# VectorE's queue in the code's order between the first and the second MoE

## The chip, the cores and the metric

The kernel runs on one core of one Trainium2 chip. The metric is the device time of one execution in microseconds (us), the median of several runs. A core has five engines with a queue each: TensorE (PE, matrix products), VectorE (DVE), ScalarE (ACT), GpSimd (POOL) and SyncE (SP, which here issues nearly all transfers). Each engine takes the instructions of its own queue one after the other, and an instruction that waits for another engine holds up what is queued behind it on the same engine.

## The reference

Four sequences of 448 positions go through attention with 12 heads of width 64, then every token through two feed-forward blocks (called MoE in the code). All tensors are float32.

```python
q_n, k_n = rmsnorm(q, g_q), rmsnorm(k, g_k)            # per head, over the 64 columns
attn = softmax(q_n @ k_n.T / sqrt(64))                 # 448 x 448
x = (attn @ v) laid out as (4 * 448 tokens, 768)
g = relu(x @ w_in) ** 2                                # w_in 768 x 2048
x = g @ w_out                                          # w_out 2048 x 768
a, b = x @ w1, x @ w2                                  # 768 x 1024
out = ((a * b) @ w3) @ moe2_w_out                      # 1024 x 1024, 1024 x 768
```

The weights arrive in 64-bit floats; the first use of each makes its float32 form on the chip and stores it for the later batches.

## The kernel before

**Numbers.** A float32 operand is held as a high part and a low part, and a product is three TensorE passes (`mm3`, L399 to L401: high by high, high by low, low by high). So every weight block ("unit", 128 x 384 or 128 x 512) and every activation needs a copy for the high part (ACT, L134) and a subtraction for the low part (POOL or DVE, L141).

**Loop over heads.** The body handles batch after batch. Iteration h of `for h in range(NH + 1)` (48 heads) emits, in this order: the first half of the scores of head h (`stage_qk`: four products, two row maxima L922 and their product L923 on DVE), exponentials on ACT (`stage_exp`, L939), transposes of the probabilities of head h-1 on PE (`stage_t`) with high parts on ACT and low parts on DVE (`stage_lo`), the parts of v (`v_prep`, vhl), the second half of the scores, the product with v (`stage_v`, its DVE sum is L1026), in every fourth iteration the norms of the next group of four heads (`group_prep`: square on ACT, sum over columns on DVE L843, then a short chain over DVE and ACT), and the operands of head h+2 (`head_prep`: kx, khl, qh, ql). Every second head ends in `stage_x` (L1032), which makes a block of the MoE's input.

**MoE work in between.** Between those stages `fill(n)` emits n TensorE passes of a running generator. In iterations 0 to 12 (batch 0's attention) that is a product of two weights (`gen_w3o`), in iterations 13 to 24 (batch 1's attention) it is `gen_moe(0)`, the MoE of batch 0, and from there on `gen_late`, the MoE of batches 1 and 2. At the end of iteration 24 the first MoE is emitted to its end by `fill(1e9)`. In the first MoE the weights are the 64-bit ones: a load of 384 or 512 KB into one of 4 buffers (raw64; SP, L309), two instructions that cut the words out (ACT L323 and POOL L329), one on DVE that joins them into float32 (L336, "join", into one of 6 raw buffers, which frees the raw64 buffer), then the high part on ACT (into one of 4 + 2 hl buffers), the low part, which frees the raw buffer, and a store of the float32 form. In the emitted order, `use(u)` emits beside the products of unit u: the load of unit u+9, the words of u+7, the join of u+6, the high part of u+5 and the low part of u+4 (`advance`, with SPLIT_AHEAD, WORD_AHEAD, JOIN_AHEAD, HI_AHEAD). The last part of the first MoE (`w3o`, 144 of its 1008 passes) needs no joins. Results of a product are taken from PSUM by a callback right after the last pass: `relu2` (r and act on ACT, gf on DVE L474, act's low part on DVE L141), `add` (L501), `gated` (L528).

**What sets the order.** The program is traced in the emitted order; a scheduler then orders every engine's queue itself, by its own estimates of when things are ready. Where the code has called `in_order(engines)`, `chain()` adds for these engines an ordering edge (it makes no wait on the chip) from each instruction to the one emitted before it on that engine, until the next call of `in_order`; the first one of such a stretch is put behind the last 300 before it. Instructions emitted after the stretch are not tied by it and may be put between. Before the change there are two stretches: SP from the end of iteration 24 on, and all five engines from the last half of the last MoE on.

Of the kernel before, what the change touches and what calls it, by code (L numbers as in the profile page):

```python
# [30 lines left out]
def attention_moe_kernel(  # L31
# [16 lines left out]
    SP, ACT, DVE, POOL, PE = (e.engine for e in (nc.sync, nc.scalar, nc.vector, nc.gpsimd, nc.tensor))  # L48
# [65 lines left out]
    def in_order(*engines):  # L114

        spans.append((nc.cur_bb.bb.instructions[-1], engines))
# [655 lines left out]
    def load_group(g):  # L772
        if not (0 <= g < NH // GH):
            return
        b, h0 = divmod(g * GH, H)
        qn = t1.tile([P, GH, C, D], F32, name="qn", tag="qn")
        kn = t2.tile([P, GH, C, D], F32, name="kn", tag="kn")
        if g == 0:
            nc.sync.dma_start(out=kn[:, 0:1], in_=k_nat[0, :, 0:1])
            load_head(0)  # L780
            nc.sync.dma_start(out=qn[:, 0:1], in_=q_nat[0, :, 0:1])
            load_to(0)
            nc.sync.dma_start(out=kn[:, 1:], in_=k_nat[0, :, 1:GH])
            nc.sync.dma_start(out=qn[:, 1:], in_=q_nat[0, :, 1:GH])
            load_to(1)
        else:
            nc.sync.dma_start(out=kn, in_=k_nat[b, :, h0:h0 + GH])
            nc.sync.dma_start(out=qn, in_=q_nat[b, :, h0:h0 + GH])
        grp[g] = [qn, kn, None, None]

    def load_head(h):
        if not (0 <= h < NH):
            return
        b, hh = divmod(h, H)
        t = t2.tile([128, S], F32, name="qt", tag="qt")
        nc.sync.dma_start(out=t, in_=q_t[b, hh])
        qts[h] = t

    def load_v(h):
        if not (0 <= h < NH):  # L800
            return
        b, hh = divmod(h, H)
        t = t2.tile([128, C, D], F32, name="v", tag="v")
        nc.sync.dma_start(out=t, in_=v_in[b, hh])
        vs[h] = t
# [103 lines left out]
    def stage_qk(h, s):  # L909
        if not (0 <= h < NH):  # L910
            return
        d = heads[h]
        nb = d["nb"] = small.tile([P, 2], F32, name="nb", tag="nb")
        c0 = 2 * s
        o = d["sc"] = [None, None]
        for j in range(2):
            c = c0 + j
            ps = ps_sc.tile([128, 512], F32, name="sc", tag="sc")
            o[j] = ps[:P, :S]
            nc.tensor.matmul(o[j], d["qh"][:, c * P:(c + 1) * P], d["kt"], start=True, stop=False)  # L920
            nc.tensor.matmul(o[j], d["ql"][:, c * P:(c + 1) * P], d["kt"], start=False, stop=True)  # L921
            nc.vector.tensor_reduce(out=nb[:, j:j + 1], in_=o[j], axis=AX.X, op=ALU.max, negate=True)  # L922
        nc.vector.tensor_tensor(out=nb, in0=nb, in1=d["rq"][:, c0:c0 + 2], op=ALU.mult)  # L923

    def stage_exp(h, s):
        if not (0 <= h < NH):
            return
        d = heads[h]
        nb, o = d.pop("nb"), d.pop("sc")
        i = h % 2  # L930
        if s == 0 and i == 0:
            sums2[h // 2] = small.tile([P, 2, C], F32, name="sm", tag="sm")
        sm = sums2[h // 2]
        c0 = 2 * s
        pp = t3.tile([P, 2, S], F32, name="p", tag="p")
        for j in range(2):
            c = c0 + j
            p = d["p"][c] = pp[:, j, :]
            nc.scalar.activation(  # L939
                out=p, in_=o[j], func=AF.Exp, scale=d["rq"][:, c:c + 1], bias=nb[:, j:j + 1],  # L940
                accum_out=sm[:, i, c:c + 1],
            )
        if h >= H:
            words = t3.tile([P, 2, S], F32R, name="pw", tag="pw")
            nc.sync.dma_start(out=words.bitcast(F32), in_=pp)
            d["p"][c0:c0 + 2] = [words[:, 0, :], words[:, 1, :]]
        if s == 1 and i == 1:
            nc.vector.tensor_scalar(out=sm, in0=sm, scalar1=1e-9, scalar2=None, op0=ALU.add)
            rs = small.tile([P, 2, C], F32, name="rs", tag="rs")
            nc.vector.reciprocal(out=rs, in_=sm)  # L950
            wide = t1.tile([P, C, 2, D], F32, name="rsw", tag="rsw")
            nc.gpsimd.tensor_scalar(
                out=wide, in0=rs.rearrange("p i c -> p c i").unsqueeze(3).to_broadcast([P, C, 2, D]),
                scalar1=1.0, scalar2=1.0, op0=ALU.mult, op1=ALU.mult,
            )
            sums2[h // 2] = wide.rearrange("p c i d -> p c (i d)")

    def stage_t(h, kc):
        if not (0 <= h < NH):
            return  # L960
        d = heads[h]
        k0, kn = KCS[kc]
        ps = ps_pt.tile([128, 512], F32, name="pt", tag="pt")
        to, one = (ps.bitcast(F32R), ident_r) if h >= H else (ps, ident)
        for c in range(C):
            nc.tensor.transpose(to[:kn, c * P:(c + 1) * P], d["p"][c][:, k0:k0 + kn], one)  # L966
        if kn == 128:
            t = t3.tile([128, 2, S], F32R, name="ptr", tag="ptr", bufs=3)
            hi, lo = t[:, 0, :], t[:, 1, :]
            d["pt"][kc] = [hi, lo]  # L970
        else:
            t = t1.tile([128, S], F32R, name="pte", tag="pte")
            hi, lo = t[:kn, :], t[kn:, :]
            d["pt"][kc] = [t]
        copy_on("a", hi, ps[:kn, :S])
        d["lo"].append((lo, ps[:kn, :S], hi.bitcast(F32)))
# [51 lines left out]
    def stage_x(h):  # L1028
        if 0 <= h < NH and h % 2:
            x = xf[0]  # L1030
            b, hh = divmod(h, H)
            nc.vector.tensor_tensor(out=x, in0=norms_to_rows(h), in1=x, op=ALU.mult)  # L1032
            late = b == B - 1 and hh // 2 in (2, 3, 4)
            t = (x2p if late else xp).tile([128, 2, S], F32R, name="x", tag="x2" if late else "x")
            copy_on("a", t[:, 0, :], x)
            sub_on("g", t[:, 1, :], x, t[:, 0, :].bitcast(F32))
            xs[b, hh // 2] = t
# [4 lines left out]
    def start_fill(gen, total):  # L1042
        state.update(gen=gen, credit=0.0, left=total)

    def fill(n):
        state["credit"] += n
        while state["gen"] is not None and state["credit"] > 0:
            try:
                k = next(state["gen"])
                state["credit"] -= k  # L1050
                state["left"] -= k
            except StopIteration:
                state["gen"] = None
# [29 lines left out]
    for h in range(NH + 1):  # L1083
        n = W3O / ((H + 1) * 6) if h <= H else (MOE / (H * 6) if h <= 2 * H else (MOE + IN) / (2 * H * 6))
        late = h > 2 * H
        if not late:
            load_head(h + 3)
            load_v(h + 1)
            if h % GH == 0:
                load_group(h // GH + 1)  # L1090
        stage_qk(h, 0)
        fill(n)
        stage_exp(h, 0)
        if late:
            load_head(h + 3)
            load_v(h + 1)
            if h % GH == GH - 1:
                load_group((h + 1) // GH + 1)
        if h % H != 1:
            stage_x(h - 2)  # L1100
        stage_t(h - 1, 0)
        stage_t(h - 1, 1)
        fill(n)
        stage_lo(h - 1)
        if h < NH:
            v_prep(h)
        fill(n)
        even = H <= h
        if even:
            stage_qk(h, 1)  # L1110
        stage_k(h + 1)
        stage_t(h - 1, 2)
        stage_t(h - 1, 3)
        fill(n)
        stage_lo(h - 1)
        if not even:
            stage_qk(h, 1)
            fill(n)
        stage_exp(h, 1)
        fill(n)  # L1120
        if even:
            fill(n)
        stage_v(h - 1)
        if h >= 2 * H and h % GH < 2:
            group_prep(h // GH + 1, "qk"[h % GH])
        elif h % GH == 1:
            group_prep(h // GH + 1)
        head_prep(h + 2)
        if h and h % H == 0:
            if h != 3 * H:  # L1130
                fill(1e9)
            stage_x(h - 1)
            if h == H:
                start_fill(gen_moe(0), MOE)
            elif h == 2 * H:
                in_order(SP)
                start_fill(gen_late(), MOE + IN)
            elif h == NH:
                start_fill(gen_pair(), MOE)
# [58 lines left out]
```

## Time and profile before

| | us |
|---|---|
| runs | 1225.1, 1224.67, 1230.58 (median 1225.1) |
| the profiled execution, its own time | 1222.35 |
| its span, first to last instruction | 1220.6 |
| busy in the span: PE | 1157.7 (95%) |
| weight loads of PE | 1036.3 (85%) |
| DVE | 856.2 (70%) |
| ACT | 728.1 (60%) |
| POOL | 719.2 (59%) |

The rows further down come from one profiled execution; times in them count from the start of its span. A busy PE is not a PE at its peak, because passes overlap: back to back, a pass of 448 columns starts about every 0.2 us and is shown with 0.36 us. The granted clock (PEclk) is 1.00 for 2.4 GHz and 0.50 for 1.2 GHz. A row of a timeline has the start, the duration, the engine, the line, the operation, output and inputs by the program's names, and in square brackets the idle time of that engine before it with the instruction that ended it. For one core, this execution is the only one shown, and its own time stands 2.75 us under the median of the runs.

### The profile page before, as it was taken

The numbers are of one execution on the slowest core, as the hardware profiler recorded it, in microseconds if no ns is written. First come the engines' busy times: TensorE is split into PE (matmuls) and PEld (weight loads), VectorE is DVE, ScalarE is ACT, GpSimd is POOL, SyncE is SP. The second block draws the span as 40 slices with busy tenths as digits, with TensorE's granted clock in tenths as the row PEclk, the third lists the DMA queues.
The fourth block names the chain that finished last, engine by engine and source line by source line (L and its number), as shares of the span: only waits on it lengthen the run. The fifth ranks groups of instructions, "written<-read, shape, count | busy, mean of one in ns | idle before, by whom it ended". The sixth has DMA issues, their size and how long they took to land.

```text
span 1220.6 us, 19049 instructions
## 1 busy us (share of the span) xinstructions
PE 1157.7 (95%) x6150; PEld 1036.3 (85%) x6150; DVE 856.2 (70%) x1441; ACT 728.1 (60%) x1586; POOL 719.2 (59%) x720
## 2 busy tenths in 40 slices
PE   7799999898898899999999999999999999999998
PEld 4588888787786789998989988889989999889998
DVE  5799879868987792766787666677564311887786
ACT  6799877767655655665664565665654535343352
POOL 6775534655675665765786756485665958521132
PEclk9699999999898999999999999999999999999999
DMA  7785648799877754565474655655545656243333
GB/s 229 233 254 162 190 129 265 244 296 265 275 243 238 233 160 152 151 196 154 148 215 133 210 156 182 206 170 168 166 139 178 188 161 193 93 124 106 121 104 117
DMA packets 122435, 224.15 MB, mean 184 GB/s; under 512 B 13440, under 2 KB 75104, under 8 KB 122336
## 3 DMA queue, kind: packets, MB, share of 16 engines
q1 hardware_dynamic: 120608, 220.19, 59.2%
q10 hardware_dynamic: 1728, 2.75, 0.6%
q8 instruction: 48, 0.79, 0.3%
q14 instruction: 51, 0.42, 0.1%
HBM read 157.03 MB, written 36.96 MB: 159 GB/s over the span
## 4 chain that ended last, share of the span: by engine, by line
PE 47%; DVE 10%; DMA 6%; ACT 4%; issue 2%; POOL 2%; SPq 0%; ACTq 0%; DVEq 0%; POOLq 0%
PE mm L399 11%; PE mm L400 11%; PE mm L401 11%; PE kv L1018 2%; PE pt L966 2%; DMA raw<-w 2%; DMA raw<-f_out 1%; DVE vhl L138 1%; DVE nb L922 1%; POOL hl L141 1%; ACT p L939 1%; PE pt L400 1%; PE pt L401 1%; PE sc L401 1%; PE sc L399 1%
## 5 line engine op out<-in xcount | busy, mean ns | idle before, releaser
L141 POOL TENSOR_TENSOR hl<-raw,hl 128x384 fp32r<-128x384 f32 (+1 forms) x317 | 372.4, 1182 | 240.1 <-ACT hl L134 210.6
L134 ACT ACTIVATE hl<-raw 128x384 fp32r<-128x384 f32 (+1 forms) x405 | 225.7, 566 | 194.0 <-PE mm L401 40.1
L400 PE MATMUL mm<-x,hl 128*128 128x448 f32 (+1 forms) x640 | 235.5, 368 | 8.9 <-POOL x L141 8.9
L399 PE MATMUL mm<-x,hl 128*128 128x448 f32 (+1 forms) x640 | 239.5, 374 | 4.6 <-DVE gf L474 2.9
L401 PE MATMUL mm<-x,hl 128*128 128x448 f32 (+1 forms) x640 | 234.1, 366 | 0.0
L400 PE MATMUL mm<-act,hl 128*128 128x448 f32 (+1 forms) x544 | 200.8, 369 | 3.5 <-POOL act L141 3.5
L399 PE MATMUL mm<-act,hl 128*128 128x448 f32 (+1 forms) x544 | 202.9, 373 | 0.0
L401 PE MATMUL mm<-act,hl 128*128 128x448 f32 (+1 forms) x544 | 198.8, 366 | 0.0
L939 ACT ACTIVATE p<-sc,nb,rr 112x448 f32<-112x448 f32 x192 | 137.5, 720 | 97.1 <-DVE nb L923 96.7
L400 PEld LDWEIGHTS mm<-x,hl 128*128 128x128 f32 x640 | 121.7, 190 | 19.7 <-POOL x L141 10.9
L399 PEld LDWEIGHTS mm<-x,hl 128*128 128x128 f32 x640 | 121.7, 190 | 15.1 <-DVE gf L474 3.4
L401 PEld LDWEIGHTS mm<-x,hl 128*128 128x128 f32 x640 | 121.7, 190 | 9.6 <-POOL hl L141 0.5
L141 DVE TENSOR_TENSOR ptr<-pt,ptr 128x448 fp32r<-128x448 f32 x144 | 87.0, 618 | 60.3 <-ACT ptr L134 59.8
L922 DVE TENSOR_REDUCE nb<-sc 112x1 f32<-112x448 f32 x192 | 113.2, 615 | 20.1 <-PE sc L921 18.8
L329 POOL TENSOR_SCALAR raw<-raw 128x384 uint32<-128x384 uint16 (+1 forms) x110 | 76.9, 699 | 77.5 <-DMA raw<-w_in 21.9
L336 DVE SCALAR_TENSOR_TENSOR raw<-raw 128x384 uint32<-128x384 uint32 (+1 forms) x120 | 89.0, 747 | 38.5 <-POOL hl L141 23.4
L400 PEld LDWEIGHTS mm<-act,hl 128*128 128x128 f32 x544 | 103.6, 190 | 14.0 <-POOL act L141 6.3
L399 PEld LDWEIGHTS mm<-act,hl 128*128 128x128 f32 x544 | 103.6, 191 | 8.2 <-ACT p L939 0.3
L401 PEld LDWEIGHTS mm<-act,hl 128*128 128x128 f32 x544 | 103.6, 190 | 7.8
L323 ACT ACTIVATE raw<-raw 128x384 f32<-128x384 f32 (+1 forms) x120 | 70.3, 598 | 58.0 <-DMA raw<-w 24.9
L920 PE MATMUL sc<-kt,qh 128*112 128x448 f32 x192 | 75.7, 394 | 19.4 <-ACT p L939 17.5
L141 POOL TENSOR_TENSOR act<-gf,act 128x448 fp32r<-128x448 f32 x64 | 80.7, 1261 | 14.5 <-ACT act L473 7.6
(151 smaller groups left out, 2197.2 us busy)
## 6 DMA issues: line engine op xcount, KB each, us to landing
pw<-p SPq DMA_DIRECT2D x72, 392.0 KB, 4.0
raw<-f_in SPq DMA_DIRECT2D x96, 192.0 KB, 3.8
raw<-f_out SPq DMA_DIRECT2D x72, 256.0 KB, 4.3
raw<-w_in SPq DMA_DIRECT2D x32, 384.0 KB, 4.5
raw<-w_out SPq DMA_DIRECT2D x24, 512.0 KB, 5.3
raw<-w SPq DMA_DIRECT2D x32, 384.0 KB, 4.4
qt<-q_t SPq DMA_DIRECT2D x48, 224.0 KB, 3.8
raw<-f SPq DMA_DIRECT2D x56, 192.0 KB, 3.8
```

Of the source, the lines that this page charges most:

```text
L134: nc.scalar.activation(out=out, in_=in_, func=AF.Copy)
L141: (nc.vector if eng == "v" else nc.gpsimd).tensor_tensor(out=out, in0=in0, in1=in1, op=op)
L323: nc.scalar.activation(out=hi, in_=hi, func=AF.Prelu, scale=2.0**-112, alpha=-(2.0**32))
L329: nc.gpsimd.tensor_scalar(out=t[:, :n, 0], in0=low, scalar1=2.0**-13, scalar2=2.0**-14 - 0.5, op0=ALU.mult, op1=ALU.add)
L336: nc.vector.scalar_tensor_tensor(out=f[:, :n].bitcast(U32), in0=t[:, :n, 1], scalar=3, in1=t[:, :n, 0], op0=ALU.logical_shift_left, op1=AL ...
L399: nc.tensor.matmul(ps, w[:, 0, wk, :], x[0], start=(i == 0), stop=False)
L400: nc.tensor.matmul(ps, w[:, 0, wk, :], x[1], start=False, stop=False)
L401: nc.tensor.matmul(ps, w[:, 1, wk, :], x[0], start=False, stop=(i == last))
L920: nc.tensor.matmul(o[j], d["qh"][:, c * P:(c + 1) * P], d["kt"], start=True, stop=False)
L922: nc.vector.tensor_reduce(out=nb[:, j:j + 1], in_=o[j], axis=AX.X, op=ALU.max, negate=True)
L939: nc.scalar.activation(out=p, in_=o[j], func=AF.Exp, scale=d["rq"][:, c:c + 1], bias=nb[:, j:j + 1], accum_out=sm[:, i, c:c + 1],)
L966: nc.tensor.transpose(to[:kn, c * P:(c + 1) * P], d["p"][c][:, k0:k0 + kn], one)
```

## The change

One more call of `in_order`, for DVE, where the first MoE starts:

```diff
             stage_x(h - 1)
             if h == H:
+                in_order(DVE)
                 start_fill(gen_moe(0), MOE)
             elif h == 2 * H:
                 in_order(SP)
                 start_fill(gen_late(), MOE + IN)
```

H is 12. A new stretch begins behind the `stage_x(11)` of iteration 12 and ends at the `in_order(SP)` of iteration 24. In it each DVE instruction is ordered behind the one emitted before it. No instruction is added or removed. The other engines' queues stay the scheduler's, which orders them anew around DVE's.

## Rows read from the trace of the kernel before

**Rows 1.** Windows: length, busy us (and count) of PE, PEld, DVE, ACT, POOL; clock, DMA share, GB/s.
```profile
192.00:442.00 250.00, 226.31 (x1182) 200.45 (x1181) 208.04 (x342) 159.55 (x351) 152.40 (x167) 0.97 0.81 251
442.00:490.00 48.00, 47.63 (x256) 43.40 (x255) 23.79 (x42) 27.07 (x60) 28.69 (x26) 1.00 0.51 155
490.00:950.00 460.00, 452.01 (x2495) 409.18 (x2494) 304.31 (x503) 274.33 (x617) 306.39 (x289) 1.00 0.57 171
```

**Rows 2.** Waits of PE, 192 to 442 us: us in total, times, longest.
```profile
PE sc L920 <- ACT p L939: 7.5, 4, 3.2
PE mm L1007 <- DVE gf L474: 4.7, 2, 2.4
PE mm L399 <- DVE gf L474: 2.9, 1, 2.9
...
PE pt L966 <- DVE ptr L141: 2.2, 4, 0.6
```

**Rows 3.** Timeline, PE and ACT, 303 to 315 us.
```profile
303.26 0.36 PE L921 MATMUL sc<-kt,ql 128*112 128x448 f32 x1
...
313.28 0.73 ACT L939 ACTIVATE p<-sc,nb,rr 112x448 f32<-112x448 f32 x1 [1.67 <-DVE nb L923]
...
314.15 0.46 PE L920 MATMUL sc<-kt,qh 128*112 128x448 f32 x1 [1.52 <-ACT p L939]
```

**Rows 4.** Timeline of DVE in the same stretch.
```profile
304.94 2.63 DVE L336 SCALAR_TENSOR_TENSOR raw<-raw 128x512 uint32<-128x512 uint32 x2
...
308.02 1.24 DVE L336 SCALAR_TENSOR_TENSOR raw<-raw 128x512 uint32<-128x512 uint32 x1
...
309.72 0.41 DVE L141 TENSOR_TENSOR khl<-kx,khl 112x256 fp32r<-112x256 f32 x1
310.06 1.21 DVE L843 TENSOR_REDUCE ss<-qn 112x16 f32<-112x1024 f32 x1
311.19 0.61 DVE L922 TENSOR_REDUCE nb<-sc 112x1 f32<-112x448 f32 x1
...
313.11 0.14 DVE L923 TENSOR_TENSOR nb<-nb,rr 112x2 f32<-112x2 f32 x1
```

**Rows 5.** Waits of DVE, 192 to 442 us.
```profile
DVE raw L336 <- POOL hl L141: 19.8, 15, 2.8
DVE ptr L141 <- ACT ptr L134: 9.5, 11, 3.0
DVE raw L336 <- POOL raw L329: 3.8, 4, 1.2
```

**Rows 6.** Windows of 25 us inside it, columns as in group 1.
```profile
317.00:342.00 25.00, 23.78 (x112) 20.93 (x112) 23.26 (x33) 14.05 (x31) 15.83 (x16) 0.88 0.77 251
...
367.00:392.00 25.00, 20.83 (x104) 18.24 (x105) 17.77 (x31) 13.93 (x32) 13.99 (x16) 0.86 0.81 229
...
417.00:442.00 25.00, 21.79 (x114) 19.39 (x113) 20.82 (x31) 14.43 (x33) 14.43 (x15) 0.93 0.60 191
```

**Rows 7.** Timeline of DVE ahead of the first MoE.
```profile
128.73 1.20 DVE L843 TENSOR_REDUCE ss<-qn 112x16 f32<-112x1024 f32 x1
...
188.14 1.14 DVE L922 TENSOR_REDUCE nb<-sc 112x1 f32<-112x448 f32 x2
...
190.49 1.22 DVE L843 TENSOR_REDUCE ss<-qn 112x16 f32<-112x1024 f32 x1
191.73 0.62 DVE L1032 TENSOR_TENSOR xf<-kv,xf 128x448 f32<-128x448 f32 x1
```

**Rows 8.** Waits of ACT, 192 to 442 us.
```profile
ACT raw L323 <- DMA raw<-w: 24.9, 15, 3.4
ACT p L939 <- DVE nb L923: 20.9, 13, 3.5
```

**Rows 9.** Waits of SP's queue, 192 to 442 us.
```profile
SPq L309 <- DVE raw L336: 65.2, 41, 4.5
```

**Rows 10.** DMA issues of the page: count, KB each, median us from issue to landing.
```profile
raw<-w_out SPq DMA_DIRECT2D x24, 512.0 KB, 5.3
```

## The prediction

> **What bounds the kernel now.** I read the windows first, then the waits of TensorE, then the timeline around some of them. From 490 us on TensorE is busy for 452.0 of 460 us at full clock. The first MoE is another matter: from 192 to 442 us TensorE is busy for 226.3 of 250 us, at a mean clock of 0.97, and DVE for 208.0, or 83%. From 442 to 490 us, where no joins are left, TensorE is back at 47.6 of 48 us and DVE at half load [rows 1]. The stretch that the change orders is these 298 us, and only its first 250 us have anything to give.
>
> TensorE's waits there nearly all end in something that DVE does late [rows 2]: the next scores wait for exponentials that free their bank (7.5 us), products wait for gf to free theirs (4.7 and 2.9), transposes for ptr (2.2). Together 17.3 us. The clock takes more: 0.88, 0.86 and 0.93 in three windows of 25 us [rows 6] are 25 x (0.12 + 0.14 + 0.07) = 8.3 us lost. One of these falls follows the wait of 1.52 us at 314.15 us [rows 3, 6].
>
> Why DVE is late can be read at that wait. The scores were done at 303.26 + 0.36 = 303.6 us [rows 3]. The row maximum that reads them starts at 311.19 and the product behind it ends at 313.25 us [rows 4]; only then come the exponentials (313.28) and TensorE's next scores. Of those 9.6 us DVE spent 5.5 us on work that stands later in the code: three joins (2.63 for two, 1.24), a khl for a later head (0.41), and the sum of squares of a group that iteration 24 prepares (1.21) [rows 4]. DVE was not slow here; its queue had the wrong thing first.
>
> The queue is also ahead of its own inputs. 15 joins stand in it before their raw buffer is free, and DVE idles 19.8 us for them, with everything behind held up [rows 5].
>
> **The change part by part.** No instruction comes or goes, so everything is a question of when.
>
> (a) Joins, khl and norms no longer overtake the row maxima, gf and ptr. At the wait above the 5.5 us leave the path, more than the 1.52 us that TensorE waited, so that wait goes. For the 17.3 us in all the ends are nothing and 17.3, and with the clock 25.6. This says what TensorE would allow: 250 - 25.6 = 224.4 us.
>
> (b) The 19.8 us of idle joins should go. The join of unit u+6 is emitted beside the products of unit u, when the low part that frees a raw buffer has been emitted for all units up to u+4. So only a few of 6 raw buffers are taken, where the scheduler's order fills all of them. Ends: nothing and all of 19.8; I take all, since buffers are left over by the code's own count.
>
> (c) DVE loses work that it now does ahead. Counted by their place in the code, 26 DVE instructions of the stretch, 15.9 us in sum, run before 191.73 us, the last DVE work of iteration 12; the first is the sum at 128.73, the last the sum at 190.49 us [rows 7]. All of them move behind 191.73 us, into the busy part. DVE's work there becomes 208.0 + 15.9 = 223.9 us. At the start the two row maxima of 188.14 us come 191.73 - 188.14 = 3.6 us later [rows 7]; the products of the first four units, whose joins are emitted ahead of the stretch, cover that, and without this cover it costs up to 3.6 us. I take 0.
>
> (d) Waits that stay or come. The ptr subtractions wait 9.5 us for ACT's copies [rows 5]; the code's order has the same pairs, so I keep them. New: gf is now emitted right behind the last pass of its product and needs ACT's r first. There are 24 such products in the stretch; the nearest ACT row is an exponential of 0.73 us [rows 3], so the ends are 0 and 24 x 0.73 = 17.5 us. Zero if DVE runs that far behind TensorE anyway, as it does by far more now [rows 3, 4]. I take 6, a third. Three norm chains pass over ACT four times each: between 0 and 3 x 4 x 0.73 = 8.8 us; I take 3. Behind a waiting gf stand the next joins and maxima, and for these wait ACT's high parts and SP's next loads.
>
> (e) SP and the loads. SP's queue waits 65.2 us for joins that free a raw64 buffer, in 41 loads, 1.6 us each [rows 9]. With joins later, loads are later. The join of a unit frees the buffer for the unit four further on, whose join is due four units later. By the code 32 + 24 + 32 = 88 units are joined, 84 of them in the stretch; over 250 us that is one in 3.0 us, so 11.9 us for four. Needed are 1.6 us on SP, 5.3 us to landing [rows 10] and about two ACT rows of 0.73 for the words: 8.4 us. 3.5 us are spare. I take 0.
>
> The sum goes by the engine that is left with the least room, DVE: 208.0 + 15.9 + 9.5 + 6 + 3 = 242.4 us for a stretch that takes 250, a gain of 7.6 us. What TensorE would allow (224.4) lies below it. The emission paces the first MoE evenly over the heads, so the last 48 us stay. Behind 490 us the schedule is made anew; TensorE idles 8 of 460 us there [rows 1], so I take 0 and keep 3 us to both sides. The profiled execution took 1222.35 us, so 1214.8 by its own time; it stands 2.75 us under the median of the runs, which gives 1217.5 us.
>
> One rule speaks against (b). The rows show the same short idle 15 times, always at a join and always ended by POOL's low part [rows 5]. The Trainium skill (Perfetto Trace Analysis, Optimization Strategy) says that a gap that repeats for a stretch on an engine that should be saturated can mean that SBUF has no room for the next tile. By that the buffers set the gap, not the order, it would come back in any order, and the sum would be 262.2 us instead of 242.4. The trace agrees that a full buffer ends those waits; that it is full in the code's order too, no row shows.
>
> **The rivals.**
>
> *Everything goes* (0.17). DVE's own lateness hides the waits of (d), so only 208.0 + 15.9 + 9.5 = 233.4 us are left, a gain of 16.6 us: 1208.5. For it: DVE now lags TensorE by 7.6 us from score to maximum [rows 3, 4]. Against: DVE would be 96% busy or waiting on ACT alone, on a chip where DMA is at 0.81 too [rows 1].
>
> *No change* (0.15). ACT keeps the scheduler's order, in which word instructions stand before their loads have landed: 24.9 us of idle for one weight alone [rows 8]. r, ptr and the exponentials queue behind them, and an ordered DVE waits for just these. The 20.9 us that ACT's exponentials wait for DVE [rows 8] then turn into DVE waiting for ACT. The upper end of gf's waits, 17.5 instead of 6, gives 253.9 us for the stretch; the middle between its ends, 8.75, gives 245.2, and halfway between these two stands 249.5: 1224.6 us.
>
> *Slower: joins that wait with attention behind them* (0.26). The place is the join. If in the code's order it still has to wait, for a raw buffer or for a load that itself waited for the join four units before, DVE can no longer do anything else, and each wait holds the next maxima and gf, so the next join too. The price of one is 19.8 / 15 = 1.3 us [rows 5]. With 7.6 us of gain, six such joins make it even; the 15 of now make 242.4 + 19.8 = 262.2, or 12.2 us more than 250: 1237 us. For it: 41 of the some 84 loads already wait for a join [rows 9], and 4 more joins wait for words [rows 5]. Against: the 3.5 us spare of (e). The repeated-gap rule above is one way into this case.
>
> That the edit does nothing is excluded: the three joins, khl and sum ahead of the maximum [rows 4] cannot stay there.
>
> **How the numbers follow.** The forecast (DVE-bound stretch, gain 3 to 12 us, 1213 to 1222) has 0.42. About 0.5%, some 6 us, is what a measurement of this kernel can tell from no change. Of the 0.42, 0.31 lie beyond it and 0.11 within. Faster: 0.31 + 0.17 = 0.48. Within: 0.11 + 0.15 + 0.02 of the slower case, with few waiting joins, = 0.28. Slower: the other 0.24. The range leaves out the end of the largest gain, below 1204 (1208.5 less the 3 us of the later part and some of the clock), and above 1238 the slower case with more than 15 waiting joins.
>
> **What would show it.** Right: from 192 us on, no row maximum later than some 3 us behind its scores; no join before a maximum whose scores are done; joins that wait for POOL's low part gone from DVE's waits; TensorE's waits for exponentials and gf under half of 17.3 us; the three clock falls fewer; DVE over 90% busy up to the last join; the norms' sums no longer before 191 us. Wrong: DVE waits for words, loads or raw buffers at joins in sum over 8 us, TensorE waiting for hl (it does not now), SP's waits for joins well above 65 us, or gf's waits for ACT over 10 us. If the stretch ends where it does now although the waits at joins are gone, (d) is the term that failed. If the stretch is shorter and the end is not, the time was lost behind 490 us.

## The result: slower by half a percent, and the profile after

| | before | after |
|---|---|---|
| median of 19 runs, us | 1227.54 | 1231.91 |
| ratio, 95% interval | | 1.0054 [1.0037, 1.0070] |
| the profiled execution, own time, us | 1222.35 | 1232.63 |

The forecast was 1217.5 us. The two profiled executions lie 10.3 us apart, the medians 4.4: the one of before was among its quick runs. So times of the two traces are compared here by stretches, and costs are taken from the ratios, at 1227 us for 1. The quotient of the two medians is 1.0036, just under the ratio's interval; so the size of the loss is less sure than its sign.

Three places where `stage_x` ends show where the time went. The last DVE work ahead of the stretch, the L1032 at 191.73 us before [rows 7], starts at 185.3 us now: the last number of this row of the instructions on xf.

```profile
L1032 DVE TENSOR_TENSOR xf<-kv,xf x6: 619/622/625, 80.2 to 185.3; 128x448 f32<-128x448 f32 x6
```

The next L1032 (two heads on) and the last one of the stretch, first in the trace of before, then in the one of after:

```profile
239.67 0.61 DVE L1032 TENSOR_TENSOR xf<-mm,xf 128x448 f32<-128x448 f32 x1
...
490.43 0.62 DVE L1032 TENSOR_TENSOR xf<-mm,xf 128x448 f32<-128x448 f32 x1
```

```profile
244.24 0.62 DVE L1032 TENSOR_TENSOR xf<-mm,xf 128x448 f32<-128x448 f32 x1
...
496.98 0.61 DVE L1032 TENSOR_TENSOR xf<-mm,xf 128x448 f32<-128x448 f32 x1
```

The kernel is 6.4 us ahead when the stretch starts, 4.6 us behind two heads later, and 6.5 us behind at its end. The stretch takes 311.7 us instead of 298.7. The stretch pays the early start back twice. The windows up to that last L1032 and from it to the last one of the stretch, first before, then after (columns as in [rows 1]):

```profile
0.00:191.73 191.73, 167.76 (x935) 140.40 (x936) 155.27 (x302) 154.88 (x342) 115.44 (x141) 0.94 0.67 202
191.73:490.43 298.70, 274.65 (x1438) 244.50 (x1438) 232.50 (x383) 186.89 (x411) 181.08 (x193) 0.97 0.76 235
```

```profile
0.00:185.32 185.32, 167.37 (x918) 141.40 (x919) 141.66 (x276) 144.57 (x321) 106.95 (x131) 0.92 0.59 181
185.32:497.00 311.68, 282.56 (x1479) 251.08 (x1479) 243.95 (x403) 202.07 (x433) 190.93 (x203) 0.97 0.77 242
```

DVE's work ahead of the stretch is 26 instructions and 13.6 us less; inside it is 11.4 us more. That the missing work is why batch 0's attention got shorter, two experiments further down bear out: with the first joins or the norms allowed ahead again, that L1032 starts at 190.7 and 188.9 us.

The same windows as in [rows 1], after (columns as there):

```profile
192.00:442.00 250.00, 222.36 (x1157) 196.57 (x1156) 211.26 (x348) 169.24 (x363) 155.92 (x172) 0.97 0.84 263
442.00:490.00 48.00, 46.52 (x246) 41.92 (x245) 21.90 (x37) 24.67 (x54) 27.56 (x25) 1.00 0.59 181
```

TensorE does 25 passes less in the 250 us than before (each trace holds 6150 in all). What it waits for has changed; waits of PE after, in the window of [rows 2]:

```profile
PE pt L966 <- DVE ptr L141: 7.4, 4, 3.1
PE kv L904 <- DVE khl L141: 5.0, 3, 2.2
PE mm L399 <- DVE gf L474: 3.4, 2, 2.5
...
PE sc L920 <- ACT p L939: 2.2, 3, 1.5
...
PE mm L401 <- DVE hl L141: 1.9, 1, 1.9
```

The wait for exponentials fell from 7.5 to 2.2 us. In its place stand ptr (2.2 to 7.4), khl (new, 5.0) and a weight's low part (new, 1.9): operands that DVE itself makes, late. Where DVE stood in the meantime is in its own waits after, which answer to [rows 5]:

```profile
DVE raw L336 <- POOL raw L329: 21.0, 17, 2.5
DVE raw L336 <- ACT raw L323: 4.3, 3, 2.1
DVE ss L843 <- ACT qn L841: 3.6, 3, 1.3
DVE rr L817 <- ACT nt L816: 2.7, 3, 1.2
DVE gf L474 <- ACT r L470: 1.1, 2, 0.7
```

The 19.8 us at joins that waited for POOL's low part are gone from the list. Joins now wait for their words, 25.3 us in 20 waits, and three norm chains wait for ACT, 6.3 us in six. ACT in turn waits for joins, which it did not before, and less for the load of w (24.9 us in [rows 8]); ACT's waits after:

```profile
ACT hl L134 <- DVE raw L336: 30.1, 28, 2.8
...
ACT raw L323 <- DMA raw<-w: 12.0, 11, 2.6
```

One norm chain in the timeline of DVE after:

```profile
210.05 1.20 DVE L843 TENSOR_REDUCE ss<-qn 112x16 f32<-112x1024 f32 x1
212.38 1.22 DVE L843 TENSOR_REDUCE ss<-qn 112x16 f32<-112x1024 f32 x1 [1.12 <-ACT qn L841]
...
215.04 0.46 DVE L817 TENSOR_TENSOR rr<-nt,rr 112x32 f32<-112x32 f32 x1 [0.56 <-ACT nt L816]
215.42 0.41 DVE L141 TENSOR_TENSOR khl<-kx,khl 112x256 fp32r<-112x256 f32 x1
...
217.07 1.14 DVE L922 TENSOR_REDUCE nb<-sc 112x1 f32<-112x448 f32 x2
...
218.83 0.55 DVE L141 TENSOR_TENSOR hl<-raw,hl 128x384 fp32r<-128x384 f32 x1
```

From 210.05 to 215.50 us DVE is held by work for heads to come. In the code the second square (ACT, L841) overwrites the tile that the first sum reads, so it waits for that sum, and the second sum waits for it. Behind the block stand khl, the row maxima and hl. TensorE after, at the same place (the scores that those maxima read, then rows that waited):

```profile
205.28 0.36 PE L921 MATMUL sc<-kt,ql 128*112 128x448 f32 x1
...
215.97 0.50 PE L904 MATMUL kv<-ident_r,khl 112*128 112x112 f32 x4 [1.22 <-DVE khl L141]
...
219.44 0.74 PE L401 MATMUL mm<-x,hl 128*128 128x448 f32 x1 [1.86 <-DVE hl L141]
```

The scores were done at 205.28 + 0.36 = 205.64 us, 11.4 us ahead of their maxima. Behind the two waits of TensorE the granted clock falls; windows after, PEclk is the third number from the end:

```profile
210.00:220.00 10.00, 6.77 (x33) 5.42 (x32) 8.11 (x18) 8.61 (x17) 4.20 (x7) 0.90 0.70 219
220.00:230.00 10.00, 10.00 (x45) 8.95 (x44) 9.85 (x16) 6.57 (x16) 4.66 (x5) 0.75 0.93 298
```

SP's queue after, which answers to [rows 9]:

```profile
SPq L309 <- DVE raw L336: 43.6, 35, 3.7
SPq L796 <- DVE ql L892: 38.3, 9, 6.0
```

The second row is new in this size: the load of a head's qt waits for ql, nine times, 4.3 us each. All weight loads stand behind it, since SP issues them from the same queue. One such place in SP's timeline after: nothing is issued from 261.5 to 267.2 us.

```profile
260.67 0.33 SPq L309 DMA_DIRECT2D raw<-w_in  x1
261.05 0.46 SPq L344 DMA_DIRECT2D f_in<-raw  x1
267.16 0.33 SPq L796 DMA_DIRECT2D qt<-q_t  x1
```

### The profile page after: what moved, and what is told of

Same layout as the page of the kernel before. It is cut to its first block, busy times and chain, and to the rows that moved or that the text cites. A ratio compares the mean times of both kernels' runs of the same rounds, so it can differ in the third digit from the quotient of the medians.

```text
span 1230.9 us, 19069 instructions
## 1 busy us (share of the span) xinstructions
PE 1166.0 (95%) x6150; PEld 1041.2 (85%) x6150; DVE 854.7 (69%) x1441; ACT 732.1 (59%) x1586; POOL 720.8 (59%) x720
## 4 chain that ended last, share of the span: by engine, by line
PE 46%; DVE 5%; DMA 3%; ACT 2%; issue 2%; POOL 1%; SPq 0%; ACTq 0%; POOLq 0%; DVEq 0%
PE mm L399 11%; PE mm L400 11%; PE mm L401 11%; PE kv L1018 2%; PE pt L966 2%; DMA raw<-f_in 1%; PE pt L400 1%; PE pt L401 1%; PE sc L399 1%; PE pt L399 1%; PE sc L400 1%; PE sc L401 1%; PE sc L921 1%; PE sc L920 1%; DMA raw<-f_out 1%
## 5 line engine op out<-in xcount | busy, mean ns | idle before, releaser
L141 POOL TENSOR_TENSOR hl<-raw,hl 128x384 fp32r<-128x384 f32 (+1 forms) x317 | 376.5, 1195 | 262.1 <-ACT hl L134 230.8
L399 PEld LDWEIGHTS mm<-act,hl 128*128 128x128 f32 x544 | 104.5, 192 | 12.2 <-ACT hl L134 2.2
L336 DVE SCALAR_TENSOR_TENSOR raw<-raw 128x384 uint32<-128x384 uint32 (+1 forms) x120 | 86.5, 731 | 35.1 <-POOL raw L329 26.7
L474 DVE TENSOR_TENSOR gf<-mm,r 128x448 f32<-128x448 f32 x64 | 39.7, 620 | 70.1 <-ACT r L470 68.0
L134 ACT ACTIVATE ptr<-pt 128x448 fp32r<-128x448 f32 x144 | 74.3, 545 | 18.7 <-PE pt L966 18.5
```

The lines of the kernel that those rows point to most:

```text
L134: nc.scalar.activation(out=out, in_=in_, func=AF.Copy)
L141: (nc.vector if eng == "v" else nc.gpsimd).tensor_tensor(out=out, in0=in0, in1=in1, op=op)
L336: nc.vector.scalar_tensor_tensor(out=f[:, :n].bitcast(U32), in0=t[:, :n, 1], scalar=3, in1=t[:, :n, 0], op0=ALU.logical_shift_left, op1=AL ...
L399: nc.tensor.matmul(ps, w[:, 0, wk, :], x[0], start=(i == 0), stop=False)
L474: nc.vector.tensor_tensor(out=gf, in0=ps, in1=r, op=ALU.mult)
```

## The experiments

Four theories. A: the norms, now in one piece of 5.5 us on an ordered DVE, cost the time. B: the joins in the code's order do, since they wait with attention behind them. C: SP stuck at qt, behind an ordered ql, makes the weights late. D came later: the joins lose a lead at the start that is never regained. Ratios are against the kernel before, timed in the same job, with 95% intervals; the changed kernel is 1.0054. The edits are made on the changed kernel unless said otherwise. A gain is a difference of two ratios and carries both intervals: some 3 to 4 us to either side, if they are independent.

**Norms out of the order.** The DVE instructions of `group_prep` are left out of the chain.

```diff
...
-                mine = [i for i in traced[:starts[m + 1]] if i.engine == e]
+                mine = [i for i in traced[:starts[m + 1]] if i.engine == e and i.name not in loose]
...
+        seen = len(nc.cur_bb.bb.instructions)
         if h >= 2 * H and h % GH < 2:
...
+        loose.update(i.name for i in nc.cur_bb.bb.instructions[seen:])
```

> The DVE instructions of the norms of a group (squares' sums L843, and the chain L810 to L817) are left out of the ordered stretch; everything else of DVE stays in the code's order. Theory A (the norm block costs the time): each of three blocks holds DVE for 5.5 to 6 us in one piece (210.0 to 215.5 us in the first), 2 of them idle on ACT, and what follows is late; without it the kernel gains 4 to 6 us on the changed kernel and comes level with the one before, ratio 0.999 to 1.002, and the waits of DVE for ACT's squares and norms (3.6 and 2.7 us) are gone. Theory B (joins that wait for their words with attention behind them): ratio stays 1.004 to 1.007, and the joins still wait 20 us or more for words. Theory C (SP held by the load of qt, 42 us, which makes the weights' loads late): the same as B, SP still over 30 us at qt.

Measured: 0.9977 [0.9959, 0.9996], faster than the kernel before. Against the changed kernel that is 0.0077, or 9.4 us, more than the 4 to 6 that theory A asked for. The waits for ACT's squares and norms, 6.3 us, are 1.9 us here (185 to 497 us). But the edit does two things at once: the block no longer stands in the order, and its work is free to run ahead again. Of the sums on qn, 13 start ahead of the last L1032 here, as in the kernel before; in the changed kernel it is 8. The joins wait less too, but they still do (lines stand one further on in this kernel; DVE's waits):

```profile
DVE raw L337 <- POOL raw L330: 13.3, 11, 3.5
```

TensorE no longer waits for khl or a weight's low part; its waits for ptr grew, from 7.4 us, and the kernel is faster even so:

```profile
PE pt L967 <- DVE ptr L142: 13.3, 8, 3.3
```

The last L1032 ahead of the stretch:

```profile
L1033 DVE TENSOR_TENSOR xf<-kv,xf x6: 615/619/625, 79.6 to 188.9; 128x448 f32<-128x448 f32 x6
```

**Joins out of the order.** The same with `loose.add(joined.ins.name)` in `join` instead.

> The joins (L336) are left out of the ordered stretch, so the scheduler may put them ahead again; the rest of DVE stays in the code's order. Theory A (norm block): no gain on the changed kernel, ratio 1.003 to 1.007. Theory B (joins in the code's order are the cost): 4 to 8 us less than the changed kernel, ratio 0.997 to 1.002, ACT's waits for joins (30.1 us) under 10. Theory C (SP held by qt): ratio 1.002 to 1.007, since qt still waits for ql in the code's order, SP over 30 us there.

Measured: 1.0121 [1.0098, 1.0144], slower still. Theory B as it was put has fallen: freeing the joins gives nothing back. A join that the scheduler may put ahead in an otherwise ordered DVE waits for POOL's low part again, and attention cannot pass it (a row of DVE's waits, its lines one further on):

```profile
DVE raw L337 <- POOL hl L142: 26.3, 21, 3.4
```

TensorE's wait for khl rises to 9.9 us in two waits. Free joins in an ordered DVE are worse than all of DVE in order and than none of it. Since they bring a wait of their own, the run does not say what the joins' order costs by itself.

**A third buffer for qt.**

```diff
-        return t2.tile([128, S], F32, name="u", tag=tag)
+        return t2.tile([128, S], F32, name="u", tag=tag, bufs=3 if tag == "qt" else 2)
...
-        t = t2.tile([128, S], F32, name="qt", tag="qt")
+        t = t2.tile([128, S], F32, name="qt", tag="qt", bufs=3)
```

> The changed kernel with a third buffer for qt, so that its load need not wait for the ql of two heads before. Theory C: SP's wait for ql goes from 42 us to under 5, the weights' loads come earlier, the joins' waits for words fall from 26 us to under 10, and the kernel gains 4 to 6 us: ratio 0.998 to 1.002. Theory A and theory B: SP's wait goes too, but the joins still come after the norm block or wait as POOL's and ACT's queues stand: ratio 1.003 to 1.007.

Measured: 1.0005 [0.9983, 1.0026], a gain of 0.0049 or 6.0 us. Theory C holds in the time, but not in each of its signs: SP's wait for ql halves and does not vanish, and the joins wait nearly as long for words as before (22.6 us, not 25.3). Waits of SP:

```profile
SPq L796 <- DVE ql L892: 18.2, 5, 6.2
```

So what the buffer gave back did not come through shorter waits at the joins; by which way it came is not shown.

**All five queues in the code's order.** `in_order(SP, ACT, DVE, POOL, PE)` in place of `in_order(DVE)`.

> All five queues in the code's order in the stretch, not DVE's alone. If the cost is that one ordered queue stands against four that the scheduler orders by its own estimates (words too late on POOL, qt too early on SP), this takes it away: joins' waits for words under 10 us, ratio under 1.000. If the cost is the code's order itself (norm block in one piece, joins just in time, theories A and B), it is as slow or slower, ratio 1.005 to 1.02, and the norm block still takes over 5 us.

Measured: 1.0270 [1.0247, 1.0292], above both of the expectations. Ordering the other four queues as well does not take the cost away: the joins wait 21.7 us for words even so. What the order of the other four costs by itself was not parted from it. SP waits longer at qt:

```profile
SPq L796 <- DVE ql L892: 52.7, 8, 10.4
```

**The third qt buffer without the order** (the same edit on the kernel before).

> The kernel before (no ordered DVE stretch) with a third buffer for qt. It tells whether the 5 us that the third buffer gave the changed kernel (ratio 1.0005 instead of 1.0054) belong to the change. Theory C (the order of DVE makes ql late, and SP sticks at qt): here SP waits only 5.4 us for ql, so nothing is gained: ratio 0.998 to 1.002. Rival (any kernel of this kind profits from the buffer): ratio 0.994 to 0.997.

Measured: 0.9995 [0.9979, 1.0011]. The buffer is worth nothing by itself; SP waits there once for ql, 4.2 us. Theory C's cost belongs to the change.

**Both: norms out, third qt buffer.**

> The changed kernel with the norms left out of the order and a third buffer for qt. If theory A and theory C are two separate costs (9 us and 6 us by the ratios 0.9977 and 1.0005 against 1.0054), they add: ratio 0.991 to 0.995, 1216 to 1221 us. If both only open the same gap (words and joins late), the second gives little: ratio 0.996 to 0.999.

Measured: 0.9932 [0.9905, 0.9959], and 0.9939 [0.9919, 0.9959] in a later job. The single gains, 0.0077 and 0.0049, make 0.0126; together they made 0.0122. So the costs look separate, and without them the ordered DVE is 7 to 8 us faster than the kernel before. The traces, one execution each, put most of it into the stretch: its last L1032 starts at 497.0 us in the changed kernel, at 488.7 with norms out, at 493.5 with the third buffer, at 484.2 and 485.8 with both. Its windows:

```profile
192.00:442.00 250.00, 229.72 (x1220) 204.74 (x1219) 215.53 (x360) 172.73 (x377) 166.53 (x179) 0.99 0.85 273
```

1220 passes in the 250 us (1207 in the trace of the later job), against 1157 in the changed kernel and 1182 before [rows 1].

**The norms in two pieces**, still in order, as the code does it from iteration 24 on.

```diff
-        if h >= 2 * H and h % GH < 2:
+        if h >= H and h % GH < 2:
             group_prep(h // GH + 1, "qk"[h % GH])
```

> The changed kernel, but the norms of a group are emitted in two pieces in two iterations (the squares and sums of q one iteration earlier), as the code does it from iteration 24 on; DVE's work in the stretch is the same but for one sum of 1.2 us. If the length of the block in one piece costs the time: the piece falls from 5.5 to about 3.5 us and the ratio to 0.999 to 1.003. If it is DVE work moved into the busy stretch that costs: as the changed kernel, ratio 1.004 to 1.007.

Measured: 1.0008 [0.9988, 1.0029], a gain of 0.0046 or 5.6 us for an edit that moves one square and one sum by an iteration. The block is 210.46 to 213.29 us, 2.8 us instead of 5.5 (DVE's timeline):

```profile
210.46 1.20 DVE L843 TENSOR_REDUCE ss<-qn 112x16 f32<-112x1024 f32 x1
...
213.10 0.19 DVE L817 TENSOR_TENSOR rr<-nt,rr 112x32 f32<-112x32 f32 x1 [0.56 <-ACT nt L816]
```

Of DVE's work only one sum leaves the stretch: 9 sums on qn start ahead of the last L1032, not 8. So of the 9.4 us that norms out gave back, 5.6 go with the length of the piece, the wait for the second square included, and not with the work; the rest, 3.8 us, is not parted.

**Only the norms tied** (on the kernel before: `group_prep`'s DVE instructions of iterations 13, 17 and 21 behind those emitted before them, nothing else ordered).

```diff
+        mine = [i for i in traced if i.engine == DVE]
+        for n, i in enumerate(mine):
+            if i.name in tied:
+                for p in mine[max(n - 300, 0):n]:
+                    tc.add_manual_dep(i, p.name, why, reason="emitted order")
...
+        if H < h < 2 * H:
+            tied.update(i.name for i in nc.cur_bb.bb.instructions[seen:])
```

> The kernel before, with nothing ordered but this: the DVE instructions of the norms of the three groups prepared in iterations 13, 17 and 21 may not run ahead of DVE instructions emitted before them. Theory A says this part alone costs: 3 to 9 us, ratio 1.002 to 1.007. If the block hurts only where the rest of DVE is in order and stands behind it, nothing: ratio 0.999 to 1.001.

Measured: 1.0033 [1.0010, 1.0055]. This part alone makes the kernel slower, by 4.0 us, less than half of the 9.4 that norms out gave back where the rest is in order behind it. TensorE waits 10.9 us for exponentials, not 7.5 (lines six further on):

```profile
PE sc L926 <- ACT p L945: 10.9, 5, 4.1
```

**All of DVE in order, norms in two pieces, third qt buffer.**

> All of DVE in the code's order, as in the changed kernel, with the two repairs that keep that order: the norms in two pieces in two iterations, and a third buffer for qt. If the two costs found (the block in one piece; SP stuck at qt) are what made the change slower, the two gains add (1.0054 to 1.0008 and to 1.0005): ratio 0.994 to 0.998, 1217 to 1222 us. If a third cost of the same size stays: ratio 0.999 to 1.002.

Measured: 0.9950 [0.9925, 0.9974]. The change as it stands, with two repairs in the code around it, is faster than the kernel before.

**The start two iterations later** (norms out, third qt buffer).

```diff
+        if h == H + 3:
+            in_order(DVE)
         stage_qk(h, 0)
...
             if h == H:
-                in_order(DVE)
```

> The kernel with norms left out and a third qt buffer (0.9932), but the ordered stretch starts with iteration 15, not 13. From the end of iteration 12 to the score sums of iteration 14 that kernel fell 9.6 us behind the one before (from 3.0 us ahead to 6.6 behind), and made up 16 after that. If this loss belongs to the place (DVE work that ran ahead of the first MoE, moved behind its start), it goes: ratio 0.986 to 0.991. If it belongs to any start of an ordered stretch (what the scheduler let run ahead has to be done in place once), it comes two iterations later: ratio 0.992 to 0.996.

Measured: 0.9889 [0.9856, 0.9922], the lowest of all.

**The first joins free** (norms out, third qt buffer, and `loose.add(joined.ins.name)` for `i < u_at[0] + 12`).

> The kernel with norms left out and a third qt buffer (0.9932), and the joins of the first units of the MoE, those that ran ahead of its start in the kernel before, left out of the order too: 8 joins, 4.4 us of DVE work, go back ahead of the start. If they are what the start costs: 3 to 6 us less, ratio 0.988 to 0.991. If their loads are no earlier use, since the raw buffers are full anyway: ratio 0.992 to 0.995.

Measured: 0.9914 [0.9887, 0.9940]. In this kernel and the one with the later start the joins' waits for words are nearly gone. A row of DVE's waits with norms out and the third buffer alone, and the same row of this kernel:

```profile
DVE raw L337 <- POOL raw L330: 14.4, 13, 3.5
```

```profile
DVE raw L337 <- POOL raw L330: 2.4, 4, 1.0
```

This made theory D: eight joins that ran ahead of the stretch's start had given the loads a lead. The time does not bear it out as plainly: 0.9914 lies inside the interval of 0.9932, though some 14 us of waits at joins are gone.

**Is the lead enough by itself?** The changed kernel, with the first joins free and nothing else.

> The changed kernel, with only this taken back: the joins of the first units of the MoE may again run ahead of its start. Theory D (the joins' waits for words come from a lead of the loads that is lost at the start and never regained): the joins' waits for words fall from 25 us to under 8, and the kernel gains 3 to 6 us: ratio 0.999 to 1.003. Rival (SP at qt and the norm block make the words late by themselves): they still wait 15 us or more, ratio 1.004 to 1.007.

Measured: 1.0062 [1.0045, 1.0079], no gain, and the waits for words are still there, though the last L1032 ahead of the stretch is back at 190.7 us:

```profile
DVE raw L337 <- POOL raw L330: 19.7, 16, 2.4
```

```profile
L1035 DVE TENSOR_TENSOR xf<-kv,xf x6: 617/621/625, 80.3 to 190.7; 128x448 f32<-128x448 f32 x6
```

So theory D in this form has fallen. With the norm block in place and SP stuck at qt the waits come in spite of the lead; which of the two brings them is not shown.

**The start, side by side.** The kernel with norms out and third buffer once more, with the start of the stretch at iteration 15 and at iteration 13, on one chip.

> Norms left out, third qt buffer, the ordered stretch from iteration 15 on, beside the same with the start at iteration 13 on one chip. Theory D: 0.986 to 0.992, and at least 0.002 under the other.

> Norms left out, third qt buffer, start at iteration 13: 0.991 to 0.995, as before. If the start costs nothing, it is level with the later start.

Measured: 0.9921 [0.9899, 0.9943] and 0.9939 [0.9919, 0.9959]. The difference, 0.0018, lies inside the intervals and under the 0.002 that theory D asked for; the first measurement had put it at 0.0043, across two jobs. What the start costs by itself stays open.

**The later start alone.**

> The changed kernel with nothing else than the start of the ordered stretch at iteration 15 in place of 13. That keeps the lead of the joins, and frees the first of the three norm blocks (and parts of the others that run early). Theory D with a third of theory A: ratio 0.996 to 1.000. If the start does not matter: a third of the norm block alone, 1.002 to 1.005.

Measured: 1.0001 [0.9982, 1.0020], between its two expectations: 0.0053 or 6.5 us under the changed kernel, with 10.9 us of waits for words at the joins (POOL's 8.8, ACT's 2.1). It frees the first norm block too, so it does not part start from block.

## Why the prediction was wrong, point by point

The steps that failed are two terms of the sum: (d), where three norm chains were taken at 3 us, and (e), where SP, and with it every wait of a join for its words, was taken at 0. In their place the runs showed 9.4 us with norms out (5.6 us with the block cut in two and kept in order), 6.0 us with the third qt buffer, and 25.3 us of waits for words at joins. With norms out and the third buffer the kernel comes to 0.9932 and 0.9939, a gain of 7.5 to 8.3 us at 1227 us, where 7.6 was forecast.

That these agree is luck, not a proof of the sum. Several of its other terms were off in both directions. And in that kernel the joins still wait 16.5 us for words (POOL's 14.4, ACT's 2.1), which in the sum would have eaten the whole gain; with the first joins free as well they wait 2.4 us, and the ratio, 0.9914, is not clearly lower. So a us of waiting on DVE was not a us of the kernel, as the sum took it to be.

(a) Attention before joins: right in kind. The wait for exponentials fell from 7.5 to 2.2 us. It was wrong that nothing else would be late: DVE's own products for TensorE (ptr, khl, hl) took the place, 14.3 us of waits, and all waits of TensorE in the window add up to 27.4 us, not 23.2. Of the other signs, waits for exponentials and gf came under half of 17.3 us (7.4); but one pair of maxima came 11.4 us behind its scores, not 3, the mean clock stayed at 0.97, and DVE was busy for 85% of the window, not over 90%.

(b) The 19.8 us at joins: that wait went, as said. By the rival reading the buffers set this gap and it would come back in any order; the trace after, with the same buffers, does not show it, so here the order set it; with the joins left free it came back (26.3 us). The Trainium skill (Perfetto Trace Analysis, Optimization Strategy) says that such a repeated gap can mean too few buffers for the next tile; here it went by order alone, from 19.8 us to none. But the sign that was written down for wrong, over 8 us of waits for words or loads at joins, came with 25.3 us. The spare 3.5 us of (e) were reckoned from the weights' own loads; the qt load that stands in the same queue was not in the sum, though a moved step's other queues belong in it.

(c) The count was right, 26 instructions (302 to 276), and the size nearly: 13.6 us left the earlier part, where 15.9 were taken, and from L1032 to L1032 DVE's work rose by 11.4. The window from 192 us shows only 211.3 us, not 223.9, since the stretch began earlier and ran slower in it. The other side had no term at all: the earlier part ended 6.4 us sooner.

(d) gf's waits for ACT: 6 taken, 1.1 measured, near the lower end. The ptr subtractions' 9.5 us are no longer in the list, against what was said. The norms: 6.3 us of idle DVE, inside the ends of 0 to 8.8. But the idle was the small part: in the sum stood only the waits for ACT, not that the block of 5.5 us stands in front of khl, maxima and hl, for two of which TensorE then waited 1.22 and 1.86 us.

The rivals: the slower one named the mechanism of the second half, joins that wait with attention behind them, 20 waits of 1.3 us; its price of 12.2 us on the stretch stands beside 13.0 measured, in part by luck, since it was added to the same sum. That freeing the joins would help fell with 1.0121. What it names as the cause, a join that waits in order, became smaller with norms out and hardly with the third buffer, and the time did not follow it. The 6.4 us gained ahead of the stretch are why the whole kernel lost less. "No change" by ACT's queue did not happen: ACT's waits for the load of w fell instead, from 24.9 [rows 8] to 12.0 us, and its waits for joins came.

What stays open: what the start of an ordered stretch costs, by which way the third buffer gains its 6 us, what makes the words late where 16.5 us of waits for them remain, and the last 3.7 us between the two profiled executions behind 497 us, which the medians do not show.

## What to carry to other kernels

In this kernel the code's order was only as good as its longest piece. Before an engine is put in such an order, look for blocks that the code emits in one go and that a scheduler had spread (here sums for later heads, 5.5 us), and cut them first. Ordering one queue also sets when the buffers it frees come free, so read the queues of the others for what will now stand at their head; here one load of another kind held all the weights. Work that ran ahead comes back where the order starts: here 26 instructions, 13.6 us. Whether the lead that it gave is missed there is not shown (0.9921 against 0.9939). And a wait on an engine is not yet time lost: here some 14 us of them went without a clear gain.

## What the runs showed that was not expected

Two edits that leave all of DVE in order, moving half a norm by an iteration (1.0054 to 1.0008) and one more buffer of 1792 bytes a partition (to 1.0005; worth nothing without the order, 0.9995), turn the change from slower to faster: 0.9950 together. The fastest kernel, norms out, third buffer, start at iteration 15, ran at 0.9889 and 0.9921, faster than both kernels compared here. And order on all engines, in a stretch where order on DVE alone can gain with these two edits, cost 2.7% without them.
